# Fused window attention and Fourier gate: batch 0's queries and keys read in six-token rows, attention output of batches 2 and 3 turned by the DMA crossbar

## The chip, the cores and the metric

The kernel runs on one core of one Trainium2 chip. The metric is device time in microseconds (us) of one execution. Three runs of the kernel before gave 176.44, 176.39 and 172.52 us (median 176.39). The profile that all rows below come from is one more execution, of 173.44 us, whose traced span is 171.7 us.

## The reference, cut to what matters

There are 4 batches, 8 heads, 768 tokens and a head width of 64; q, k and v are float32. A query sees the first 8 keys of its sequence (global) and the 96 keys up to its own position (local), with a distance bias per head. The output feeds a second block of width 512.

```python
# attention, per batch and head
scores = q @ k.T / 8 - slope[h] * dist        # kept: key < 8, or 0 <= query - key < 96
a = softmax(scores);  x = a @ v               # x: [4, 768, 512] once heads are joined
# second block
x1, x2, x3 = split(x @ w_proj, 3)             # three projections of width 512
conv = irfft(rfft(x2, axis=1) * rfft(filter_fft, axis=1))    # over the 768 tokens
out = (x1 * conv * x3) @ w_out
```

## The kernel before, in words

**Attention.** The 768 tokens of a batch are cut into seven key tiles of 128 rows. Rows 0 to 7 of a tile repeat the 8 global keys, the other 120 are the tile's own; the last tile starts at token 648 and so overlaps the sixth. A key tile meets at most 216 queries. The tiles form three groups `c`: (0, 1), (2, 3), (4, 5, 6). Heads are handled in four pairs, 64 partitions to each head.

For batches 1 to 3, GpSimd (POOL) issues one DMA per tile of q, k or v, which also turns float32 into float16 (`load_rows`, `load_q`, line 322). Each row of a head is a piece of its own, of 256 bytes in DRAM: 960 pieces for a k or v tile, 1,024 for one of the six q tiles of 128 rows. The global rows are copied by DMAs that SyncE (SP) issues. There is one buffer each for `qn` and `kn`, so a batch's loads wait until the batch before has been transposed out of them; `vn` has two. For batch 0, SP loads q as float32 into the output staging tiles `ot`, and TensorE transposes it as float32 (`turned32`, line 639).

Scores need q and k with the head width on the partitions. `turned` (line 652) does that with TensorE transposes against an identity, and ScalarE (ACT) or VectorE (DVE) moves the result from PSUM into `QT` and `KT`. Batch 3 (`CROSS`) has it done by the DMA crossbar instead, with nine transposing DMAs on SP (`crossed`, lines 626 and 629). Then come score matmuls (line 693), the exponential on ACT (707, 12 to a batch), the mask product on DVE (724; in batch 0 the bias is added by matmuls instead, 684), the value matmuls (742 and 747, 65 columns, where the 65th is the sum of the weights), the reciprocal (771) and the scaling into `xn` (766 on DVE, or 770 on ACT).

`transpose_x` turns `xn` into `xT`, tokens along the free axis: TensorE transposes (787), and ACT or DVE copies 480 or 576 columns out of PSUM (306). That makes two groups of transposes and two copies per group `c`, 24 copies in all.

**Second block.** `gate` multiplies `xT` by the outer thirds of `w_proj` (856, four matmuls of 384 columns to a gate) and keeps x1·x3 in `g`. `butterfly` forms sums and differences of the three token thirds on DVE (801 to 812). `conv` projects them (925), goes to the spectrum (613), multiplies by the filter on DVE (1076 to 1096), comes back (950, 953), joins the halves (1033 to 1052), multiplies by `g` (1056) and projects out (977) into `ot`, which SP stores (985).

**Order.** Nothing is scheduled at build time or on the chip. The text `ORDER` lists every operation by number, with its engine (P, V, A, G, S) and, for matmuls, the PSUM banks it takes, and each engine executes its own sequence of it in order. An operation whose data are late holds up everything behind it on its engine. Batches overlap: while batch b is in its second block, batch b+1 is loaded, scored and weighted. Matmuls on zeros (`busy`, line 302) fill the wait at the start.

Of the kernel before, what the change touches and what calls it, by code (L numbers as in the profile page):

```python
# [39 lines left out]
0V 42V 3V 7V 27S 59S 28S 60S 61S 26S 69S 4G 54A 48A 45A 56A 50A 5V 1V 6V 29G 30G 66G 33G 65G 77G i6b1 17P0 18A  # L40
58A 47A 46A 43A 19V 11V 12P1 13A 49A 44A 57A 2A 14V 8V 15V 16A 55A 53A 20V 34V 39A 21A 51A 52A 22A 36A 37A 10V
40V 35G 70G 71G 72G 32G 68G 67G 73G i15b3 120P2 121V 9V 41V 93P3 94A 97P1 98V 82V 38V 258G 31G 74G 75G 267G
266G 226P0 95P4 96A 99A 230A 100P5 i1b6 122P2 123A 87A i1b1 126P3 127V 231V 269G i2b1 124P4 125V 101V 62V 64V
229V 268G 257G 255G 256G 259G 79G 76G 78G 80G 81G 262G i2b1 128P67 129A 134P23 135A 91P1 92V 24V 63V 132P45
133A 130P67 131A 102P23 103A 168P1 169V 227V 106P45 107A 170P6 171V 232V 166P7 167A 172P1 173V 228V 25V 261S
260S 263S 264S 275G 274G 273G 272G 265G 104P23 105A 108P45 109A 176P67 177A 178P01 179A 86A 136P23 137V 138V
141P45 142V 143V 174P67 175A 83A 115P23 116V 117V 110P01 111V 112V 180P45 181A 139P6 140A 89A 88A 144P7 145V
182P23 183V 184V 118P0 119A 85A 113P1 114V 187P45 188V 189V 383P7 185P6 186A 84A 384A 385P2 386V 213V 152P3
190P4 191V 212V 219V 215V 220V 357P6 147P2 149A 358A 154A 355P5 356V 198P4 200A 90A 359P2 360V 222V 214V 488G
271G 270G 496G 487G 489S 484G 495G 485G 193P7 195A 162P3 164A 396P01 397A 398V 216V 221V 364P45 361P67 362A  # L50
365A 208P2 210A 151P3 153V 366V 223V 23V 224V 225V 217V 146P0 148A 161P1 163A 165V 150V 218V 157P4 159A 370P67
393P23 394A 395V 367P01 368A 371A 192P5 194V 369V 372V 196V 156P4 158A 160V 155V 363V 233V 234V 235V 236V 237V
238V 239V 297P2 295P3 296A 387P01 388A 298A 390P67 280P4 281A 293P3 294A 391A 207P0 299P1 308P2 309A 300A
306P3 307A 301P5 203P4 205A 302A 284P2 285A 431P1 429P3 430A 432A 202P4 204V 209V 433P5 434A 490S 504G 486G
277G 503G 501G 276G 278G 506G 502G 494G 498G 378P67 379V 380V 392V 389V 252P23 253A 254A 240P4 241V 244P1 245A
246P5 247A 248P67 250A 249A 242P0 243A 373P23 374V 375V 206V 211V 719G 282P1 435P45 436A 283A 399P67 400V 401V
251V 441P23 442A 197P0 199A 404P45 405V 310V 406V 722G 491G 493S 720S 492S 381P1 382V 376P6 377A 288P7 289A
402P2 403V 443V 286P0 287A 583P3 407P4 408A 585P5 586V 437V 290V 584V 291V 303V 438P67 439A 440V 304V 292V
444P01 587P2 588A 445A 446V 311V 715G 717S 716G 409P4 419P5 410P6 412A 421A 420P7 595P23 596A 422A 598P01 599A
425P6 424P5 426A 427A 411A 447P23 448V 305V 449V 611P7 612A 723G 497G 279G 452P01 453V 454V 728G 505G 714G  # L60
500G 659P6 660A 324P5 314P4 315A 320P7 321V 428V 600V 312P2 316P3 317A 325A 313A 450P6 661P4 662A 318P0 455P3
456V 423V 201V 451V 478V 477V 413V 597V 479V 326P5 327A 319A 322P7 415P1 417A 323A 589P23 592P45 593A 811S
414P6 416A 468P0 470A 590A 458P1 460A 613P7 614V 418V 480V 328V 329V 481V 482V 594V 330V 483V 331V 591V 332V
457P6 459A 657P0 658A 729G 507G 734G 713G 712G 499G 730G 726G 727G 725G 732G 731G 724G 735G 733G 473P2 475A
618P45 619A 620V 333V 335V 621P67 615P01 616A 622A 463P3 472P2 474A 462P4 464A 465A 512P5 513A 521P6 522A
669P01 670A 624P23 625A 626V 525P7 526A 523P6 524A 672P45 663P01 664A 508P2 509A 673A 601P67 602V 334V 603V
623V 336V 665V 617V 671V 510P3 511A 467P0 536P1 537A 666P45 667A 668V 838S 718S 814S 813S 812S 837S 882S 721S
839S 883S 340P2 341A 469A 514P1 516P3 517A 515A 632P67 604P2 534P0 535A 538V 633V 674V 527P4 528A 605A 343P3
344A 606P01 607V 634V 608V 518V 352P5 353A 354S 529P4 530A 675P23 676V 519V 471V 635P5 636A 677A 627P67 609P4
610V 680P01 681V 628V 629V 532V 682V 531V 539V 520V 533V 346P5 337P4 338A 347A 339S 345S 342S 348S 349P6 630P7  # L70
631A 821P23 824P01 825A 350A 822A 351S 678P4 679V 826V 683P5 638P7 640A 684A 705V 653P0 548P6 546P1 547A 549A
550P2 544P3 554P7 555A 551A 545A 552P4 553V 706V 708V 707V 466V 461V 709V 476V 542P1 543A 655A 686P5 688A
691P4 693A 643P2 645A 540P3 541A 556V 843P67 840P01 841A 849P45 850A 647P2 649V 637P3 639A 844A 652P0 654V
823V 557V 558V 710V 559V 842V 560V 641V 711V 701P1 703A 893P45 846P23 847A 894A 815P67 736P0 737A 816A 817V
648P1 650A 749P2 890P45 891A 750A 696P3 698A 762P0 763A 832P67 833V 563V 651V 834V 561V 848V 892V 564V 753P1
754A 642P4 644A 751P5 752A 887P23 888A 884P01 818P67 819A 820V 845V 851V 895V 656V 740P4 741A 764P5 738P2 739A
885A 765A 766V 695P3 697A 700P4 742P2 743A 827P67 828V 829V 889V 886V 562V 757P0 758A 580P5 581A 702A 744P1
685P0 687A 755P5 756A 830P4 831A 745A 857P23 858V 859A 896P67 897V 898V 901P45 902V 903A 746V 747V 760V 689V
568P0 565P1 852P67 853V 854V 759V 748V 767V 571P2 572A 577P3 578A 860P4 690P5 861V 761V 835P2 836A 566A 855P3
856A 904P6 905A 899P7 900V 927V 926V 646V 929V 928V 930V 931V 704V 932V 574P2 575A 576S 567S 573S 582S 768P1  # L80
782P4 770P6 771A 569A 570S 579S 774P3 780P2 778P7 779A 783A 769A 868P6 776P0 777A 775A 772P7 773A 781A 784V
785V 786V 699V 787V 788V 791V 862P4 950P1 951A 933P7 934A 692A 694V 789V 792V 937P0 948P1 949A 938A 946P5
935P7 936A 947A 954P1 955A 867P0 952P3 959P5 961P7 962A 869A 953A 960A 872P1 874V 957V 956V 958V 963V 964V
941P2 942A 864A 870A 917P7 939P0 940A 943V 944V 945V 802P1 803A 805P5 878P6 863P4 865A 877P0 980P1 981V 866V
790V 971P4 972A 919A 879A 880A 808P3 984P4 978P2 982P7 983A 979A 967P1 968V 985V 986V 965P0 966A 969P6 970A
973V 881V 974V 975V 987V 976V 988V 977V 1004V 989V 799P7 793P4 794A 800A 801S 795S 804S 873P6 875A 809A 876V
871V 916P2 918A 796P1 797A 991V 990V 992V 993V 994V 920V 1006V 798S 810S 921P4 912P0 914A 911P3 913A 806A 923A
807S 922P2 906P1 908A 924A 925V 915V 907P3 909A 910V 1007V 1005V 1001P0 1002A 1003S 995P1 996A 997S 998P2 999A
1000S 1008P0 1009V 1010S 1014P1 1015V 1016S 1011P3 1012A 1013S
# [108 lines left out]
class Fused:  # L198
# [11 lines left out]
    CROSS = (3,)  # L210
    LATER = ()
# [8 lines left out]
    def __init__(self, ctx, tc, q, k, v, n_global, n_local, w_proj, filt, w_out, out):  # L220
# [10 lines left out]
        self.K0 = [KL * t for t in range(6)] + [S - KL]  # L231
# [6 lines left out]
    def buffers(self):  # L238
# [5 lines left out]
        self.qn = t("qn", [P, 6, H, D])  # L244
        self.kn = t("kn", [P, 7, H, D])
        self.vn = [t(f"vn{i}", [P, 7, H, self.VD]) for i in range(2)]
        self.QT = t("QT", [P, 4, S])
# [4 lines left out]
        self.xn = [t(f"xn{i}", [P, 2, 7, 2, D]) for i in range(2)]  # L252
# [12 lines left out]
        self.h1 = t("h1", [P, 6, DM])  # L265
        self.h2 = t("h2", [P, 6, DM])
# [24 lines left out]
        self.wide_dg = self.mix.bitcast(BF16).rearrange("p a b c -> p (a b c)")[:, 0:648]  # L291
        self.cst = t("cst", [1, 4])
        self.one = t("one", [1, P])
# [31 lines left out]
    def load_rows(self, what, dst, src, b, t):  # L325

        lo, hi = self.K0[t], self.K0[t] + KL
        self.load("G", dst[P - (hi - lo):P, t, :, 0:self.D],
                  src[b, :, lo:hi, :].rearrange("h p d -> p h d"), [what + (t,)], (8 * (hi - lo), 256),
                  f"load{what}{t}")  # L330

    def load_run(self, what, dst, src, t, n):

        rows = src[0, :, self.K0[t]:self.K0[t] + KL * n, :].rearrange("h (t p) d -> p t h d", t=n)
        self.load("G", dst[NG:P, t:t + n, :, 0:self.D], rows, [what + (i,) for i in range(t, t + n)],
                  (8 * KL * n, 256), f"load{what}{t}")

    def load_q(self, b, t):
        src = self.q[b, :, P * t:P * t + P, :].rearrange("h p d -> p h d")
        if b == 0:  # L340
            st = self.ot[t].rearrange("p (h d) -> p h d", h=self.H)
            self.load("S", st, src, [("ot", t)], (1024, 256), f"q{t}")
            if self.Q32:
                return
            self.g.op("AV", {"A": act(512), "V": 0.7}, lambda e: self.copy(
# [26 lines left out]
    def setup(self):  # L372
# [6 lines left out]
        def rows(_):  # L379
            row = self.row  # L380
            v.memset(row[:, 4, 0:1], 0.0)
            for n in (1, 2, 4, 8, 16, 32, 64):
                v.tensor_scalar(row[:, 4, n:2 * n], row[:, 4, 0:n], float(n), None, op0=Alu.add)
# [857 lines left out]
```

## Time and profile before

| what | value |
|---|---|
| profiled execution / its traced span | 173.44 us / 171.7 us |
| TensorE matmuls (PE), busy share of the span | 162.3 us, 95% |
| VectorE (DVE) | 156.7 us, 91% |
| ScalarE (ACT) | 151.1 us, 88% |
| GpSimd (POOL) | 77.4 us, 45% |
| first exponential / last of batch 0's value matmuls | 17.5 us / 29.8 us |
| first projection of batch 3 | 138.4 us |
| end of the last matmul / last copy out of PSUM starts | 167.8 us / 167.9 us |

A row of the groups reads: line, engine, operation, out<-in, partitions x elements and type, how often, then busy us and mean ns of one, and the idle time in front. A row of the chain reads: start, duration, engine, output and line. Instructions of one engine overlap a little at their ends, and matmuls a lot: one of 128 columns is recorded with 219 ns, while the chain has six of them in 0.34 us. So the cost of a matmul is read from the chain, and the sum of ACT or DVE durations is slightly more than the time they take. The PE's busy share counts a matmul until its result is out and is higher than the share in which it streams columns.

### The profile page before, as it was taken

The page shows a single profiled execution, that of the slowest core. Times are in us where ns is not written, and L with a number is a line of the kernel's source. Part 1 is how long each engine was busy: PE and PEld are TensorE (multiplying, and loading weights), DVE is VectorE, ACT ScalarE, POOL GpSimd, SP SyncE. Part 2 cuts the span into 40 slices and gives each one's busy share as a digit, 9 for nine tenths or more (in the row PEclk, how much of TensorE's full clock was granted, in tenths as well). Part 3 has the DMA queues.
Part 4 walks back from the last instruction along what each step waited for, and adds up shares of the span by engine and source line. Part 5 has one row for each costly group of instructions (what it writes and reads, how often), then busy time and mean ns, then how long its engine had stood idle before and what let it go on. Part 6 is the DMA issues. An engine that isn't in the chain of part 4 may idle for free.

```text
span 171.7 us, 4390 instructions
## 1 busy us (share of the span) xinstructions
PE 162.3 (95%) x1675; PEld 102.2 (60%) x1675; DVE 156.7 (91%) x355; ACT 151.1 (88%) x309; POOL 77.4 (45%) x95
## 2 busy tenths in 40 slices
PE   6888899999999979999999999999999999999990
PEld 1365689865464757965455767654576745575540
DVE  7997989989999899999999998999989999999960
ACT  5799999999899979999999999999998986866841
POOL 8999999962499994948993000000000000000000
PEclk9999999999999999999999999999999999999999
DMA  6999999999999999999999996500000360000854
GB/s 127 181 207 151 144 154 146 169 203 187 148 151 142 144 144 135 87 140 137 156 151 134 153 188 199 230 4 0 0 4 0 117 256 0 0 0 28 308 217 186
DMA packets 98077, 22.44 MB, mean 131 GB/s; under 512 B 90808, under 2 KB 94984, under 8 KB 98056
## 3 DMA queue, kind: packets, MB, share of 16 engines
q0 software_dynamic: 80912, 12.14, 100.3%
q1 hardware_dynamic: 17144, 10.02, 22.2%
q8 instruction: 13, 0.21, 0.5%
q14 instruction: 8, 0.07, 0.1%
HBM read 25.84 MB, written 6.29 MB: 187 GB/s over the span
## 4 chain that ended last, share of the span: by engine, by line
PE 72%; DMA 6%; POOL 6%; DVE 6%; ACT 6%; issue 2%; ACTq 0%; DVEq 0%
PE bank L856 23%; PE bank L925 9%; PE bank L977 9%; PE bank L950 5%; PE bank L693 5%; PE bank L613 5%; PE bank L652 4%; DMA QT<-qn 3%; PE bank L787 3%; PE bank L742 3%; DMA qn<-in_q_dram 3%; POOL kn L322 3%; PE bank L747 3%; POOL vn L322 2%; PE bank L684 2%
## 5 line engine op out<-in xcount | busy, mean ns | idle before, releaser
L856 PE MATMUL bank<-xT,w 128*128 128x384 f16 x256 | 47.4, 326 | 0.0
L707 ACT ACTIVATE E<-bank 128x864 f16<-128x864 f32 x48 | 41.4, 917 | 0.7 <-ACT h L310 0.3
L856 PEld LDWEIGHTS <-w 128*128 128x128 f16 x256 | 23.8, 98 | 16.3 <-issue 1.1
L322 POOL DMA_DIRECT2D vn<-in_v_dram x28 | 25.7, 923 | 4.4 <-DMA g<-in_moe_filter_fft_dram 3.9
L322 POOL DMA_DIRECT2D kn<-in_k_dram x28 | 25.9, 934 | 2.7 <-PE bank L856 2.2
L977 PE MATMUL bank<-wo,y 128*128 128x512 f16 x96 | 22.8, 379 | 0.0
L724 DVE TENSOR_TENSOR E<-E,mask 128x864 f16<-128x864 f16 x36 | 20.8, 603 | 0.8 <-ACT E L707 0.8
L322 POOL DMA_DIRECT2D qn<-in_q_dram x18 | 16.3, 917 | 6.1 <-PE bank L652 5.6
L310 ACT ACTIVATE ot<-bank 128x512 f32<-128x512 f32 x22 | 13.3, 618 | 4.6 <-PE bank L977 4.0
L866 ACT CAST g<-bank 128x384 f16<-128x384 f32 x32 | 15.9, 536 | 1.1 <-PE bank L856 0.9
L310 ACT ACTIVATE ab<-bank 128x512 f16<-128x512 f32 x24 | 14.2, 619 | 2.6 <-PE bank L925 2.5
L766 DVE TENSOR_TENSOR xn<-bank,rc 128x512 f16<-128x512 f32 (+1 forms) x21 | 16.0, 764 | 0.5
L742 PE MATMUL bank<-vn,E 128*128 128x65 f16 x224 | 15.3, 193 | 0.0
L742 PEld LDWEIGHTS <-E 128*128 128x128 f16 x224 | 14.0, 97 | 1.9
L747 PE MATMUL bank<-vn,E 128*128 128x65 f16 x192 | 15.1, 193 | 0.0
L977 PEld LDWEIGHTS <-y 128*128 128x128 f16 x96 | 8.9, 98 | 9.3 <-DVE y L1056 0.2
L693 PE MATMUL bank<-QT,KT 64*128 64x216 f16 (+2 forms) x224 | 13.9, 241 | 0.3 <-DMA QT<-qn 0.3
L306 ACT CAST X<-bank 128x512 f16<-128x512 f32 x24 | 13.6, 610 | 0.6 <-PE bank L613 0.5
L310 ACT ACTIVATE x<-bank 128x384 f16<-128x384 f32 x25 | 12.5, 526 | 1.3 <-DVE g L868 1.0
L747 PEld LDWEIGHTS <-E 128*128 128x128 f16 x192 | 13.2, 97 | 0.5
L306 ACT CAST eo<-bank 128x384 f16<-128x384 f32 x27 | 11.5, 508 | 1.4 <-PE bank L953 1.4
L693 PEld LDWEIGHTS <-KT 64*128 64x128 f16 x224 | 8.5, 94 | 6.3 <-issue 4.4
(142 smaller groups left out, 354.8 us busy)
## 6 DMA issues: line engine op xcount, KB each, us to landing
out_dram<-ot SPq DMA_DIRECT2D x24, 256.0 KB
kn<-in_k_dram POOLq DMA_DIRECT2D x28, 120.0 KB, 5.4
vn<-in_v_dram POOLq DMA_DIRECT2D x28, 120.0 KB, 5.2
qn<-in_q_dram POOLq DMA_DIRECT2D x18, 128.0 KB, 5.3
ot<-in_q_dram SPq DMA_DIRECT2D x6, 256.0 KB
w<-in_moe_w_proj_dram POOLq DMA_DIRECT2D x4, 256.0 KB, 6.7
g<-in_moe_filter_fft_dram POOLq DMA_DIRECT2D x1, 768.0 KB, 14.1
w<-in_moe_w_proj_dram POOLq DMA_DIRECT2D x1, 512.0 KB, 9.4
```

The lines of the kernel that those rows point to most:

```text
L306: {"A": nc.scalar.copy, "V": nc.vector.tensor_copy, "G": nc.gpsimd.tensor_copy}[e](out, in_)
L310: self.nc.scalar.mul(out, in_, c)
L322: return self.g.op(eng, 0.57 + 0.00035 * nbytes[0] if eng == "G" else 0.5, lambda _: e.dma_start(dst, src), w=w, r=r, nbytes=nbytes, name= ...
L693: nc.tensor.matmul(bs[hh].f32()[:, off:off + w], self.KT[hs, m, hp], self.QT[hs, hp, KL * m:KL * m + w], start=(off == 0 and not near), st ...
L707: g.op("A", act(864), lambda _: nc.scalar.activation(eo, bs[0].two()[:, :, 0:432].rearrange("p h (m w) -> p h m w", m=2), Act.Exp, scale=s ...
L724: g.op("V", dve(864, 2), lambda _: nc.vector.tensor_mul(eo, eo, mk), r=[("mask", 2 * hp), ("mask", 2 * hp + 1)], w=[("E", hp, gi)], name=" ...
L742: nc.tensor.matmul(o[:, n, hh], ef[:, at:at + P], vt[:, t, 2 * hp + hh, 0:D + 1], start=first, stop=(t == 0), skip_group_check=True)
L747: nc.tensor.matmul(o[:, n, hh], ef[:, at:at + P], vt[:, t - 1, 2 * hp + hh, 0:D + 1], start=False, stop=True, skip_group_check=True)
L766: nc.vector.tensor_mul(to, o[:, :, :, 0:D], rc.to_broadcast([P, 2, 2 * nt, D]))
L856: nc.tensor.matmul(bk.f32()[:, 0:h], self.w[:, c, o + P * j:o + P * j + P], self.xT[:, c, h * s:h * s + h], start=(c == 0), stop=(c == 3))
L866: g.op("A", act(h), lambda _: nc.scalar.copy(x3, pts[1].f32()[:, 0:h]), use=[pts[1]], w=[ko], name="x3")
L977: nc.tensor.matmul(bk.f32(), y[:, c, P * t:P * t + P], self.wo[:, c, :], start=(c == 0), stop=(c == 3))
```

## The change

1. **Batch 0's q and k** arrive in eight DMAs on POOL, one for each head pair of q and of k. Partition p gets tokens 6p to 6p+5 of two heads, so a piece is 1,536 bytes of DRAM instead of 256 (`load_six`). `six` transposes each pair with 12 TensorE transposes, 64 data columns each, and two copies put the columns back in token order in `QT` or `KT`, with steps of six elements. SP's six q loads, the float32 transposes and the seven k loads of 120 rows go.
2. **Tiles of 48 rows.** The last k and v tile holds only tokens 720 to 767. q is tiled like k, seven tiles of 120 and 48 rows, and `QT` has the layout of `KT`. A score matmul that ran over 216 or 168 queries is now two, of 120 and of 96 or 48.
3. **Crossbar for `xn`.** In batches 2 and 3 (`XX`) TensorE's transposes and the copies out of PSUM go. `xn` is one tile, laid out for it, and SP issues one transposing DMA per token tile, seven to a batch (`crossed_x`). The scaling into `xn` on DVE takes two instructions in place of one. The next batch's scaling waits until the crossing of the same group has read `xn`.
4. Batch 3's nine crossings of q and k are four (`QX`, `KX`).
5. **Setup.** The index rows are made by 9 instead of 16 small DVE instructions; the slope tables by 8 products of 128 rows on ACT and DVE instead of 16 of 64 rows on ACT; one activation table load goes; the memsets on `vn` and `kn` shrink.
6. The last output tile is made in two halves of 256 columns. The filter spectrum is kept in smaller tiles.
7. `ORDER` is new throughout: the filter and batch 0's spectrum work stand earlier, 14 instead of 27 matmuls on zeros are left, and much of the rest has moved.

```diff
+    XX = (2, 3)
-        self.K0 = [KL * t for t in range(6)] + [S - KL]
+        self.K0 = [KL * t for t in range(6)] + [S - 48]
...
+    def load_six(self, what, dst, src, i):
+        self.load("G", dst[:, i], src[0, 2 * i:2 * i + 2].rearrange("h (p r) d -> p h r d", r=6),
+                  [(what + "six", i)], (256, 1536), f"six{what}{i}")
...
-    def turned32(self, t):
+    def six(self, what, i):
...
+            for r in range(6):
+                for hh in range(2):
+                    nc.tensor.transpose(b.f16()[64 * hh:64 * hh + 64, P * r:P * r + P], buf[:, r, hh], self.ident)
...
+        def move(e):
+            self.copy(e, dst[:, 0:6, i, lo:lo + KL].rearrange("p m (c r) -> p r m c", r=6),
+                      view(0, 120).rearrange("p r (m c) -> p r m c", m=6))
+            self.copy(e, dst[:, 6, i, end[0]:end[1]].rearrange("p (c r) -> p r c", r=6), view(120, P))
...
-                for hh in range(2):
-                    hs = slice(64 * hh, 64 * hh + 64)
-                    nc.tensor.matmul(bs[hh].f32()[:, off:off + w], self.KT[hs, m, hp],
-                                     self.QT[hs, hp, KL * m:KL * m + w], ...)
+                for x in range(1 + (w > KL)):
+                    n = w - KL if x else min(w, KL)
+                    for hh in range(2):
+                        hs = slice(64 * hh, 64 * hh + 64)
+                        nc.tensor.matmul(bs[hh].f32()[:, off + KL * x:off + KL * x + n], self.KT[hs, m, hp],
+                                         self.QT[hs, m + x, hp, 0:n], ...)
...
+    def crossed_x(self, c):
+        for t in self.GRP[c]:
+            at, n = KL * t - 8 * (t % 2), (P if t % 2 else P - 16) if t < 6 else 48
+            self.g.op("S", 1.25, lambda _, at=at, n=n, t=t: self.nc.sync.dma_start(
+                self.xT[:, :, at:at + n], self.xn[0:n, t].rearrange("p h d -> p (h d)"), transpose=True),
+                nbytes=(4 * n, 256), name="crossx", r=[("xn", j, c) for j in range(2)],
+                w=[("xT", j, c, t) for j in range(2)])
...
             for j in range(2):
                 self.values(j, c, b % 2)
-                self.transpose_x(j, c)
+                if b not in self.XX:
+                    self.transpose_x(j, c)
+            if b in self.XX:
+                self.crossed_x(c)
...
+            for lo, hi in ((0, 256), (256, 512)) if last and t == 5 and self.HALVES else ((0, 512),):
```

## The prediction

> **What bounds the kernel now.** I read the page's engine shares first, then the busy time by stretches, then the chain that ended last, and the groups by shape for prices.
>
> ```profile
> PE 162.3 (95%) x1675; PEld 102.2 (60%) x1675; DVE 156.7 (91%) x355; ACT 151.1 (88%) x309; POOL 77.4 (45%) x95
> ```
>
> Three engines are nearly full, so no single one can be named from the page. The stretches (length; then busy us of PE, weight loads, DVE, ACT, POOL; granted clock; DMA share; GB/s) part them:
>
> ```profile
> 40.00:50.00 10.00, 10.00 (x74) 5.36 (x74) 9.83 (x22) 9.52 (x18) 5.70 (x7) 1.00 2.10 159
> 120.00:130.00 10.00, 10.00 (x133) 6.50 (x132) 9.33 (x20) 9.60 (x30) 0.00 (x0) 1.00 0.01 2
> 150.00:160.00 10.00, 10.00 (x74) 6.37 (x72) 9.71 (x25) 6.10 (x15) 0.00 (x0) 1.00 0.16 61
> ```
>
> In the middle DVE and ACT, which empty PSUM, are busy 93 to 98%; what is taken off both shortens it. The PE's full marks there are recorded latencies: 133 matmuls in the second row, most of them of 65 columns, cannot fill 10 us at the 30 ns at which such matmuls follow each other. After 138 us ACT has slack, and the chain is PE without a break:
>
> ```profile
> 77.42 0.24 PE bank L652 x4
> ...
> 86.16 2.66 POOL kn L322 x3
> 88.82 5.37 DMA qn<-in_q_dram
> 94.19 5.77 DMA QT<-qn
> 100.09 0.55 PE bank L693 x8
> ...
> 138.36 5.18 PE bank L925 x24
> ...
> 158.71 3.90 PE bank L856 x24
> 162.62 5.19 PE bank L977 x24
> 167.88 0.60 ACT ot L310
> ```
>
> This also gives true prices: 216 ns for 512 columns (L977, L925), 163 ns for 384 (L856), 55 to 60 ns for a 128-column transpose (L652). The 77 to 100 us pieces say that batch 3's first scores wait for its loads, one after another on POOL, and then for the crossbar.
>
> **The change part by part.**
>
> *Front, to the first exponential.* ACT is the engine that is late here: from 5.2 us on it hardly stops until the first exponential.
>
> ```profile
> 1.76 1.28 ACT L310 ACT_TABLE_LOAD   x1 [1.76 <-DVE eo L381]
> 17.50 4.78 ACT L707 ACTIVATE E<-bank 128x864 f16<-128x864 f32 x6
> ```
>
> By the new order, ahead of that point ACT loses one table load (1.28 us), 12 of 16 slope products (3.4 us for 16, so 2.6), two spreads of the distance table (0.7), one table copy (0.5), three q casts (590 ns each less overlap, 1.5), one k copy (0.3) and one mask (0.7): 7.6. It gains four pairs of six-step copies, 720 and 48 columns. No row shows a stepped copy on either engine; the nearest, 576 columns at 696 ns and 1,024 at 1,017 ns, give 0.8 for 720, and 64x64 at 248 ns gives 0.2 for 48. That is 3.0 with overlap taken off to 4.0 without, and four more table and first-row copies at 0.4 each, 1.6. Net -2.0 to -3.0. The first angle matmul, which waited for the index rows until 4.78 us, also comes sooner. Against it stand the loads: POOL issues eight pair loads of 256 pieces. A load of 960 pieces costs it 0.93 us, one of 512 pieces (w) 0.82, so 256 cost some 0.75; with 4.2 us of distance tables in between, the last pair is issued at about 11.6 us, and at 5.4 us to landing arrives at 17. Three pairs are there by 12, enough to start. Values of batch 0 are then issued from 15 to 23 us instead of 13.6 to 20.7, with the filter ahead of them. I take -2.0; the bounds are 0 (the loads decide) and -3.6.
>
> *Transposes of batch 0.* 24 float32 and 28 float16 transposes go (24 x 0.11 + 28 x 0.056 = 4.2 us), 96 with half the output partitions come. The nearest row is line 460, four of this shape in 0.30 us with 0.22 us latency: 28 to 56 ns each, 2.7 to 5.4. Zero net on a PE that waits for ACT here.
>
> *Scores.* 192 more matmuls, the same columns. Pairs for two heads run side by side (eight of 216 columns in 0.48 us with latency). If every short one cost the 29 ns of a 65-column matmul, the sum would be 5.6 us of PE; if columns count, 0. They stand where PE waits for exponentials, and are hidden by those; without that cover 5.6 is their price. I take 0.
>
> *Crossbar for xn.* The copies that go, half of these rows:
>
> ```profile
> L306 ACT COPY xT<-bank 128x480 f16<-128x480 f16 x10 | 5.9, 585 | 2.1 <-PE bank L787 2.1
> L306 ACT COPY xT<-bank 128x576 f16<-128x576 f16 x3 | 2.1, 696 | 0.0
> L306 DVE COPY xT<-bank 128x480 f16<-128x480 f16 x6 | 2.3, 400 | 0.0
> L306 DVE COPY xT<-bank 128x576 f16<-128x576 f16 x5 | 2.3, 454 | 0.2 <-ACT eo L306 0.2
> L766 DVE TENSOR_TENSOR xn<-bank,rc 128x512 f16<-128x512 f32 x15 | 10.2, 687 | 0.3
> L766 DVE TENSOR_TENSOR xn<-bank,rc 128x768 f16<-128x768 f32 x6 | 5.7, 957 | 0.1
> ```
>
> Six on ACT (5 x 0.585 + 0.696 = 3.6) and six on DVE (3 x 0.400 + 3 x 0.454 = 2.6): 6.2 us. The scaling on DVE in two parts pays its fixed cost twice: from the two L766 rows, 0.15 us plus 1.05 ns an element, over eight groups that is 1.2 us, less 0.7 for one group that goes to ACT, where four more small products cost 0.9. Seven q tiles instead of six make copies of batches 1 and 2 longer, 0.7. Net 6.2 - 0.5 - 0.9 - 0.7 = 4.1 over two engines that share their work, so -2.0. The 56 PE transposes (3.1 us) lie behind these engines and count nothing. What comes is SP's time:
>
> ```profile
> L629 SPq DMA_TRANSPOSE QT<-qn x6: 1192/1515/2042, 88.9 to 103.5; - x6
> ```
>
> Seven per batch take 8 to 14 us of SP, and the last of a group lands some 1 us after its issue ends. A group of three is thus ready 5 to 7 us after `xn`, where transposes and copies took 1.5 to 2. In the new order, counted with these rows, 11 us of other DVE work stand between the last reciprocal of batch 3 and its butterfly (before, 4.7), so I count the latency at nothing; uncovered it costs 3 to 5 us a batch. Behind a crossing on SP stand later crossings and output stores; six staging tiles hide the stores. The added wait, scaling of batch 3 until batch 2's crossing has read `xn`, would hold all of DVE; batch 2's crossings are a whole batch older.
>
> The Trainium skill, "VectorE: DVE Perf Modes", section "The three transpose paths", speaks against this step: it lists 390 ns for a 128x128 transpose on TensorE, 1309 ns by DMA, and advises TensorE where PSUM will do. By that figure 28 blocks a batch would take an estimated 37 us, which no cover could hide; the row above has four blocks in 1.2 to 2.0.
>
> *Tail.* From 138.36 us the chain holds 29.5 us of PE: all the projections, spectrum and output of batch 3, 24 output matmuls of batch 2, and 56 gate matmuls left over. The new order has 40 gate matmuls after that point: 16 x 0.163 = 2.6 less. They run earlier, where PE has gaps; half of it may only move, so -1.3 (0 to -2.6). The half-size last copy (0.60 against about 0.4) gives -0.2.
>
> *Loads.* POOL issues as long as before: 60 of 120 rows, 10 of 48 (about 0.78), 8 pairs, 68.4 us against 74 x 0.92 = 68.1. Nothing, up to -1 where buffers come free sooner.
>
> **The sum.** -2.0 - 2.0 - 1.3 - 0.2 = -5.5. Against the profiled execution, 173.44 us, that is **168.0 us**. That execution lies 1.7% under the median of the runs shown, 176.39; two of three lie there, so a median may come out up to 3 us higher for the same work. Two per cent is about what a measurement here can tell from nothing.
>
> **Rivals.**
>
> *The loads take the front back (no change).* For: POOL waits 5.6 us for qn's transposes in the trace, and batch 3 starts on loads; batch 0's values are now issued 2 us later, the gates' weights after them. Against: scores start on three pairs. Without the front's -2.0 and the tail's -1.3 the time is 171.3. The shorter front decides nothing if the first gate stays at its present 31 us.
>
> *The crossings come late (slower).* Batch 2's last three crossings stand on SP behind batch 3's crossings of 16 and 20 blocks, which wait for loads that end now at 94 to 99 us. If those end no sooner, they follow at about 102.5, take 3 x 2.04 + 1 = 7.1, and the butterfly, at 103.8 now, starts at 109.6: +5.8. With the same 3 to 5 us uncovered in batch 3, the time is 168.0 + 5.8 + 5 = 178.8. It is slower than before once the two delays exceed 5.5 us in sum, and over 2% slower from 9.
>
> *The change does less than it says.* Stepped copies at twice the price (8 x 0.8 = 6.4 us over two engines, +3.2) and the short score matmuls at half their bound (+2.8) would give 174.0: no change.
>
> **How the numbers follow.** The forecast's case, 164 to 170, has 0.62. No change, from the first and third rival, has 0.24; late crossings 0.14. All gains at their bounds are 3.6 + 4.1 + 2.6 + 0.2 + 1 = 11.5, or 162. The range runs from 163 to 176: it takes in the no-change cases and the higher median, and leaves out most of late crossings and the very end of the gains.
>
> **What would show it.** Right: first exponential near 15.5 us; first projection of batch 3 near 134; a last stretch of 27 us of PE; fewer than 0.5 us of DVE idle before the butterflies of batches 2 and 3. Wrong: DVE or PE idle released by DMA xT<-xn, PE idle before batch 0's values or first gates released by loads, stepped copies over 1 us. The prediction fails if SP's queue, not DVE and ACT, sets the middle.

## The result and the profile after

The change makes the kernel slower: 181.89 us median (180.54 to 182.6) against 174.45 of the kernel before on the same chip, a ratio of 1.054 with a 95% interval of 1.042 to 1.066. Some executions of one and the same kernel are 1 to 3% slower than its others, and every ratio here is taken from the faster ones of both kernels, so it can differ from the quotient of the two medians beside it. The forecast was 168.0, with 176 as the upper end. The profiled execution took 181.34 us, its span 179.5.

The first two lines of the page of the changed kernel (busy time of each engine; granted TensorE clock in 40 slices):

```profile
PE 163.1 (91%) x1854; PEld 104.0 (58%) x1854; DVE 157.8 (88%) x361; ACT 154.6 (86%) x299; POOL 75.3 (42%) x99
...
PEclk9995555999999999999999999999999999999999
```

The shares are lower only because the span is longer: DVE and ACT, from which work was to be taken, are each busy for more us than before (156.7 and 151.1). The clock is at half in four slices of the front. Its stretches, in the columns shown for the kernel before:

```profile
10.00:20.00 10.00, 3.40 (x66) 2.71 (x60) 3.33 (x17) 9.96 (x14) 8.69 (x11) 0.69 1.32 154
20.00:30.00 10.00, 8.08 (x117) 6.66 (x114) 9.88 (x13) 8.44 (x11) 7.59 (x10) 0.50 2.11 157
...
120.00:130.00 10.00, 10.00 (x110) 5.46 (x105) 9.66 (x18) 9.61 (x17) 0.00 (x0) 1.00 0.28 107
```

From 10 to 20 us ACT is full, DVE is busy a third of the time and TensorE a third; in the kernel before, the same stretch had 8.07 us of TensorE and 8.37 of DVE beside 9.89 of ACT. From 20 to 30 us DVE is full with 13 instructions. That is nearly 0.8 us each. From 120 to 130 us both are as full as they were. The groups by shape over the first 40 us name what fills them in the front:

```profile
L314 ACT COPY KT<-bank 128x720 f16<-128x720 f16 x2 | 5.2, 2582 | 0.5 <-PE bank L651 0.5
L314 ACT COPY QT<-bank 128x720 f16<-128x720 f16 x2 | 5.1, 2544 | 0.0
L314 DVE COPY KT<-bank 128x720 f16<-128x720 f16 x2 | 5.2, 2606 | 0.0
L314 DVE COPY QT<-bank 128x720 f16<-128x720 f16 x2 | 5.1, 2560 | 0.0
...
L314 ACT COPY KT<-bank 128x48 f16<-128x48 f16 x2 | 1.1, 552 | 0.0
```

A stepped copy (one that writes every sixth place) of 720 columns takes 2.54 to 2.61 us where the prediction put 0.8, on both engines alike, and one of 48 takes 0.45 to 0.55 in place of 0.2. The timeline of ACT (start, length) has the first exponential at 24.4 us, 17.5 before:

```profile
23.10 1.28 ACT L727 ACT_TABLE_LOAD   x1
24.40 1.89 ACT L727 ACTIVATE E<-bank 128x864 f16<-128x864 f32 x2
```

The chain that ended last carries the copies one after another, then two pieces of the middle, then the tail:

```profile
12.69 2.62 ACT KT L314 x2
...
16.71 2.61 ACT QT L314 x2
...
20.33 2.69 DVE KT L314 x4
23.02 2.63 DVE QT L314 x2
26.30 2.73 DVE QT L314 x2
29.05 2.61 DVE KT L314 x3
...
92.04 11.67 DMA QT<-qn
...
148.61 5.18 PE bank L965 x24
...
170.92 4.33 PE bank L1020 x20
...
175.81 0.71 ACT ot L318 x2
```

Read along the two kernels (start of the same work, before and after): first exponential 17.5 and 24.4; last reciprocal of batch 0 at 30.3 and 41.4; batch 1's first projection copy at 82.2 and 88.0; batch 3's first exponential 100.7 and 104.25; batch 3's first projection 138.4 and 148.6; span 171.7 and 179.5. The front loses 11 us, and the tail gains 2.3 (29.5 us from that projection to the last copy, now 27.2). The marks between do not say where the rest is won or lost, because the new order puts other work between them: from batch 3's first exponential to its first projection there are 88 gate and 44 output matmuls where there were 72 and 24, which is 6.9 us of TensorE at 0.163 and 0.216 us each, and that stretch is 6.7 us longer.

The copies that went are gone as forecast. These groups answer to the `xT` and `xn` rows of before:

```profile
L314 ACT COPY xT<-bank 128x480 f16<-128x480 f16 x5 | 2.9, 571 | 0.3 <-PE bank L816 0.3
L314 ACT COPY xT<-bank 128x576 f16<-128x576 f16 x2 | 1.3, 660 | 0.0
L795 DVE TENSOR_TENSOR xn<-bank,rc 128x256 f16<-128x256 f32 x10 | 3.7, 413 | 0.1
L795 DVE TENSOR_TENSOR xn<-bank,rc 128x384 f16<-128x384 f32 x6 | 2.9, 540 | 0.0
```

### The profile page after: what moved, and what is told of

The parts are those of the page before. It is cut to its first block, busy times and chain, and to the rows that moved or that the text cites. A ratio compares the mean times of both kernels' runs of the same rounds, so it can differ in the third digit from the quotient of the medians.

```text
span 179.5 us, 4745 instructions
## 1 busy us (share of the span) xinstructions
PE 163.1 (91%) x1854; PEld 104.0 (58%) x1854; DVE 157.8 (88%) x361; ACT 154.6 (86%) x299; POOL 75.3 (42%) x99
## 4 chain that ended last, share of the span: by engine, by line
PE 72%; DVE 12%; DMA 7%; ACT 6%; issue 2%; ACTq 0%
PE bank L893 21%; PE bank L1020 11%; PE bank L965 9%; DMA QT<-qn 7%; PE bank L990 5%; PE bank L616 4%; PE bank L714 4%; PE bank L678 4%; PE bank L310 3%; DVE QT L314 3%; PE bank L764 3%; DVE KT L314 3%; PE bank L769 3%; ACT KT L314 2%; PE bank L816 2%
## 5 line engine op out<-in xcount | busy, mean ns | idle before, releaser
L330 POOL DMA_DIRECT2D kn<-in_k_dram x25 | 21.5, 863 | 10.8 <-PE bank L678 9.0
L330 POOL DMA_DIRECT2D qn<-in_q_dram x25 | 21.4, 859 | 7.7 <-PE bank L616 4.3
L1020 PE MATMUL bank<-wo,y 128*128 128x512 f16 (+1 forms) x100 | 22.9, 371 | 0.0
L318 ACT ACTIVATE ot<-bank 128x512 f32<-128x512 f32 (+1 forms) x24 | 13.7, 593 | 4.8 <-PE bank L1020 4.2
L714 PEld LDWEIGHTS <-KT 64*128 64x128 f16 x416 | 12.5, 100 | 8.6 <-issue 7.4
L714 PE MATMUL bank<-QT,KT 64*128 64x120 f16 (+2 forms) x416 | 16.1, 214 | 1.5 <-DMA QT<-qn 1.3
L314 ACT CAST eo<-bank 128x384 f16<-128x384 f32 x30 | 13.4, 519 | 2.9 <-issue 1.6
L318 ACT ACTIVATE x<-bank 128x384 f16<-128x384 f32 x28 | 14.0, 533 | 0.3 <-PE bank L893 0.2
L314 ACT CAST X<-bank 128x512 f16<-128x512 f32 x21 | 11.6, 629 | 0.2 <-PE bank L616 0.2
L990 PE MATMUL bank<-inv,X 128*128 128x256 f16 x64 | 11.2, 272 | 0.0
```

The costliest lines, as they stand in the source:

```text
L314: {"A": nc.scalar.copy, "V": nc.vector.tensor_copy, "G": nc.gpsimd.tensor_copy}[e](out, in_)
L318: self.nc.scalar.mul(out, in_, c)
L330: return self.g.op(eng, 0.57 + 0.00035 * nbytes[0] if eng == "G" else 0.5, lambda _: e.dma_start(dst, src), w=w, r=r, nbytes=nbytes, name= ...
L714: nc.tensor.matmul(bs[hh].f32()[:, off + KL * x:off + KL * x + n], self.KT[hs, m, hp], self.QT[hs, m + x, hp, 0:n], start=(off == 0 and x ...
L990: nc.tensor.matmul(o[:, 0:P] if z else o[:, P:3 * P], X[:, s, cs], self.inr[:, s - 4] if z else self.inv[:, (s + 2) % 4], start=(n == 0), ...
L1020: nc.tensor.matmul(bk.f32()[:, 0:hi - lo], y[:, c, P * t:P * t + P], self.wo[:, c, lo:hi], start=(c == 0), stop=(c == 3))
```

## The experiments

Two theories stood first. A: the price of the stepped copies is the loss. B: the late crossings and the new order are, and the front's delay would be swallowed anyway.

### What the stepped copies cost

**Plain copies.** In `six`, the copies run through both sides in order, which leaves batch 0's tokens mixed up:

```diff
-            self.copy(e, dst[:, 0:6, i, lo:lo + KL].rearrange("p m (c r) -> p r m c", r=6),
-                      view(0, 120).rearrange("p r (m c) -> p r m c", m=6))
+            self.copy(e, dst[:, 0:6, i, lo:lo + KL], b.f16()[:, 0:720].rearrange("p (m c) -> p m c", m=6))
...
```

> The changed kernel, with the eight pairs of copies of batch 0 reading and writing runs of 120 and 48 columns in place of steps of six. It leaves out the putting back of batch 0's queries and keys into token order, so that their attention is taken between mixed-up tokens; loads, matmuls, order and sizes stay. Theory A (the stepped copies are what the change loses): the copies fall from 2.57 us to 0.7 to 0.8 and from 0.5 to about 0.35, the first exponential comes at 16 to 18 us instead of 24.4, batch 0's attention ends 8 to 11 us sooner, and the time falls from 181.9 to 170 to 174. Rival B (the late crossings and the new order lose it, and the front's delay would be swallowed later anyway, as half of it is by batch 2): the time stays at 177 or more.

Measured: 172.87 us against 172.89, a ratio of 0.991 (0.985 to 0.996). The first exponential came at 16.4, and the copies took 0.75 us on ACT and 0.53 on DVE:

```profile
L314 ACT COPY QT<-bank 128x720 f16<-128x720 f16 x2 | 1.5, 748 | 0.0
L314 DVE COPY QT<-bank 128x720 f16<-128x720 f16 x2 | 1.1, 528 | 0.0
```

Theory A stands, with 9 us by the medians and 11 by the ratios; B falls as the main cause.

**The loops exchanged.** The write is dense now (to neighbouring places), and the read of PSUM jumps 256 bytes from element to element; all is computed:

```diff
-            self.copy(e, dst[:, 0:6, i, lo:lo + KL].rearrange("p m (c r) -> p r m c", r=6),
-                      view(0, 120).rearrange("p r (m c) -> p r m c", m=6))
+            self.copy(e, dst[:, 0:6, i, lo:lo + KL].rearrange("p m (c r) -> p m c r", r=6),
+                      view(0, 120).rearrange("p r (m c) -> p m c r", m=6))
...
```

> The changed kernel, computing all, with the two loops of the stepped copies exchanged: the write goes through neighbouring 2-byte places, the read of PSUM jumps by 256 bytes from element to element. If the step of the write to SBUF sets the price (2-byte pieces 12 bytes apart), the copies fall to 0.8 us or near it. If any access that does not run through neighbouring places costs this much, whichever side it is on, they stay at about 2.5 us, and the time at 180 to 183. If PSUM is worse than SBUF at it, they cost over 3 us.

> The changed kernel with the copies' loops exchanged, computing all, for a time with an interval. One run gave 172.9 beside 172.9 before. The prediction's sum without its misprice would be 168 to 169, a ratio of 0.97; if the crossings eat the middle, it stays within 1% of before, 0.985 to 1.0.

Measured: 172.9 in the single run; then, repeated, 172.07 against 174.02, a ratio of 0.983 (0.978 to 0.989). Its groups by shape:

```profile
L314 DVE COPY QT<-bank 128x720 f16<-128x720 f16 x2 | 1.8, 902 | 0.0
L314 DVE COPY KT<-bank 128x720 f16<-128x720 f16 x2 | 1.8, 900 | 0.0
L314 ACT COPY KT<-bank 128x720 f16<-128x720 f16 x2 | 1.5, 759 | 0.5 <-PE bank L651 0.5
L314 ACT COPY QT<-bank 128x720 f16<-128x720 f16 x2 | 1.5, 748 | 0.0
```

The same elements, moved to the same places: 0.75 and 0.90 us in place of 2.55. The step of the read costs ACT nothing (0.75 with plain copies too) and DVE 0.37 us; the step of the write is what costs. This version is 6 to 7% faster than the change and 1 to 2% faster than the kernel before (0.983 here, 0.990 in a later run).

**A price by step.** The changed kernel with dense reads and other steps of the write:

```diff
...
+            n = {"q0": 2, "k0": 4, "q2": 8, "k2": 12, "q1": 2, "k1": 4, "q3": 8, "k3": 12}[what + str(i)]
+            self.copy(e, dst[:, 0:6, i, lo:lo + KL].rearrange("p m (c r) -> p r m c", r=n),
+                      b.f16()[:, 0:720].rearrange("p (r m c) -> p r m c", m=6, r=n))
```

> The changed kernel with the eight 720-column copies reading PSUM densely and writing 2-byte places at steps of 2, 4, 8 and 12 elements (4, 8, 16 and 24 bytes), one of each on ACT and on DVE; it leaves out the right token order of batch 0. If every jump of the write costs the same, all eight take about 2.55 us. If the price follows the number of new 16-byte lines that are entered (the Trainium skill, page "SBUF — State Buffer", says that leaving a line pays, without a price), steps of 4 bytes cost about a quarter of the extra 1.8 us, 1.2 us, steps of 8 bytes 1.6 to 1.7, and 16 and 24 bytes the most and alike, about 2.5 to 3.2.

Groups by shape, each in the stretch of one copy, so that steps are not mixed; in this order, on ACT steps of 24, 8, 4 and 16 bytes, and on DVE of 8, 4, 16 and 24:

```profile
L314 ACT COPY KT<-bank 128x720 f16<-128x720 f16 x1 | 3.3, 3329 | 0.5 <-PE bank L651 0.5
L314 ACT COPY KT<-bank 128x720 f16<-128x720 f16 x1 | 1.8, 1786 | 0.0
L314 ACT COPY QT<-bank 128x720 f16<-128x720 f16 x1 | 0.9, 948 | 0.0
L314 ACT COPY QT<-bank 128x720 f16<-128x720 f16 x1 | 3.3, 3340 | 0.0
L314 DVE COPY KT<-bank 128x720 f16<-128x720 f16 x1 | 1.7, 1748 | 0.0
L314 DVE COPY QT<-bank 128x720 f16<-128x720 f16 x1 | 0.9, 949 | 0.0
L314 DVE COPY QT<-bank 128x720 f16<-128x720 f16 x1 | 3.4, 3371 | 0.0
L314 DVE COPY KT<-bank 128x720 f16<-128x720 f16 x1 | 3.4, 3418 | 0.0
```

The price grows with the step up to 16 bytes and stays there at 24. It fits a price for each 16-byte line entered: 720 writes at 4 bytes enter 180 of them, at 16 bytes 720, so (3.34 - 0.95) / 540 = 4.43 ns a line, and 0.15 us remain. From these two, 8 bytes (360 lines) come to 1.75 and 12 bytes (540 lines) to 2.54: measured 1.75 to 1.79, and 2.54 to 2.61 in the changed kernel. The 48-column copies do not lie on this line: 36 lines would make 0.31 us, and they took 0.45 to 0.55. The expectation by lines was right in form; its figures were 0.25 us high at 4 bytes and at least 0.15 low at 16. The Trainium skill, "SBUF — State Buffer", section "Specifications (TRN2)", has the rule: 16-byte lines, at least two hits on each for full speed, a penalty for each crossing. It gives no price; these rows do, and they do not show its threshold: at 8 bytes each line gets two hits and the copy takes 1.75 to 1.79 us, at 4 bytes it gets four and the copy takes 0.95.

**The step on TensorE's side.** Products with the identity write float32 PSUM at every sixth place of two banks, and the copies read it densely:

```diff
-                    nc.tensor.transpose(b.f16()[64 * hh:64 * hh + 64, P * r:P * r + P], buf[:, r, hh], self.ident)
+                    for bk, lo, n in ((b, 0, 60), (b2, 60, 68)):
+                        nc.tensor.matmul(bk.f32()[64 * hh:64 * hh + 64, r:6 * n:6], buf[:, r, hh],
+                                         self.ident[:, lo:lo + n], start=True, stop=True, skip_group_check=True)
```

> The changed kernel, computing all, with the step moved from the copies to TensorE: products with the identity write float32 PSUM at every sixth place over two banks (60 and 68 columns each, 24 matmuls for 12 transposes), and the copies read dense runs of 360. Theory A: copies of 0.75 to 0.85 us, the time as with plain copies, 170 to 174, unless TensorE writes stepped columns slowly; 192 matmuls of 64 columns at 30 ns are 0.72 us for each group of 24, and over 2 us a group would mean that the step costs there too. Rival B: 177 or more.

Measured: 175.74 against 172.89, 1.014 (1.008 to 1.021). 24 matmuls took 0.86 us, 12 whole transposes 0.53, so no price of the stepped write into PSUM shows beside the number of matmuls; 24 dense ones were not run. The copies took 0.75 and 0.90. Better than the change, but above A's range of 170 to 174 (and under B's 177): by the ratios 2% behind the plain copies and 3% behind the exchanged loops, with copies as long as theirs. Why was not settled.

**The half clock.** 33 idle matmuls more, in TensorE's waits between 10 and 25 us:

```diff
-... 207P0 ... 89P3 ... 84P1 ... 94P3 ...
+... i7b6 207P0 ... i7b6 89P3 ... i14b6 84P1 ... i5b6 94P3 ...
```

> The changed kernel with its stepped copies as they are, and 33 more idle matmuls of 512 columns in the waits of TensorE between 10 and 25 us, where its granted clock is 0.5. If the copies themselves set the front, nothing moves, 180.5 to 182.5, though the clock shows 1.0. If the half clock is a good part of the loss (scores of batch 0 at 0.9 us a pair in place of 0.55, the exponentials waiting for them), 177 to 179.5.

Measured: 179.98 against 173.72, 1.040 (1.034 to 1.046), between the two expectations. The stretches of this run:

```profile
10.00:20.00 10.00, 9.02 (x94) 4.76 (x90) 3.95 (x17) 9.96 (x14) 8.64 (x11) 1.00 1.31 157
20.00:30.00 10.00, 5.72 (x123) 4.32 (x120) 9.90 (x13) 9.26 (x11) 7.34 (x9) 1.00 2.10 159
```

The clock is at 1.00 and the copies are as full as ever: the first exponential came at 24.4 again, batch 0's last reciprocal at 41.1 (41.4 without). So the half clock went with TensorE's waiting (3.40 us busy from 10 to 20 us, 9.02 here) and cost the front 0.3 us at most. This ratio is 1.4% under the change's, but the two intervals overlap, and no more is read from it.

### What the crossbar is worth

**Without it.** The changed kernel, with turns and copies of batches 2 and 3 back on TensorE, DVE and ACT; each turn is put two matmul groups behind its scaling, or behind the last gate that still reads the old `xT`:

```diff
-    XX = (2, 3)
+    XX = ()
```

> The changed kernel with its front as it is, but xn of batches 2 and 3 turned by TensorE and copied by ACT and DVE again, as in batches 0 and 1, in an order in which each turn stands two matmul groups behind its scaling. Theory A: the front's loss stays and the crossbar's gain goes, 182 to 185. Rival B (late crossings lose it): b2's butterfly comes 8 us or more sooner than at 120 us, and the time falls under 177.

> The same without the crossbar for xn in either batch. Prediction's term: 2 us more than with it, 174.5 to 176. Rival (the crossbar costs as much as it gives): 171 to 173. With the copies' loops as the change has them, leaving the crossbar out gave 191.3 against 181.9; if that order of turns is what costs and not the copies, this run comes out 8 to 10 us above 172.9 too, and the gap opens behind xT copies.

> The changed kernel with the copies' loops exchanged, and xn of batch 2 turned by TensorE again; only batch 3 uses the crossbar, when no loads are under way. Prediction's term: DVE and ACT get 3 us of copies back, 1.5 us slower, 174 to 175. Rival (crossings of batch 2 run beside batch 3's loads and hold them up): the first crossing of batch 3's queries lands in 6 to 8 us in place of 12.9, the gap of PE and ACT at 90 to 105 us closes, and the time is 169 to 172.

Measured: 191.28 against 172.89 with the stepped copies (1.108, 1.103 to 1.114). With the loops exchanged, 181.75 against 173.72 without any crossing (1.049, 1.042 to 1.056) and 179.71 with batch 3 alone crossed (1.039, 1.032 to 1.045); with both it was 0.983. All three are slower than either theory's figure. They are no clean price, since turns that have to wait for late gates of the batch before stand in TensorE's queue in an order made for crossings. But one reading is clean: in the run with batch 3 alone, no crossing of `xn` stands beside the first crossing of batch 3's queries, and this still landed after 12.43 us (11.91 in the run with stepped copies and no crossing of `xn` at all, 11.7 to 12.9 with both batches crossed). So the crossings of `xn` are not what makes that one late. What the crossbar is worth in the changed kernel stays open.

**The crossbar part alone.** The kernel before, with the new layout of `xn`, the shifted values and `crossed_x` for batches 2 and 3, each transfer put on SP's queue as soon as its scalings are done, and nothing else moved:

```diff
+    XX = (2, 3)
...
-                self.transpose_x(j, c)
+                if b not in self.XX:
+                    self.transpose_x(j, c)
+            if b in self.XX:
+                self.crossed_x(c)
```

> The kernel before, with one part of the change alone: xn of batches 2 and 3 laid out by tokens and turned by the crossbar, each group's transfers issued on SP's queue as soon as both scalings are done, nothing else moved; the 24 turns and copies go. The prediction's term: 6.2 us of copies less 2.1 of dearer scaling over two engines, 2 us faster, so 170.5 to 171.5 against 172.9. Rival (crossings and loads share the DMA engines: in the last kernels the first crossing of batch 3's queries took 12.9 us to land, 5.8 in the kernel before): batch 3's first scores wait 4 to 7 us longer, the butterflies of batches 2 and 3 wait for xT by 2 us or more each, and the time is 176 to 182.

Measured: 191.39 against 173.72, 1.110 (1.100 to 1.120), far above even the rival's 176 to 182. The waits name it, in us in total, times, longest:

```profile
DVE xab L816 <- DMA xT<-xn: 13.2, 1, 13.2
...
DVE xab L818 <- DMA xT<-xn: 5.2, 1, 5.2
```

and the chain shows what batch 2's crossings stood behind:

```profile
100.04 1.32 SPq L627
101.48 1.20 SPq L627
102.77 1.21 SPq L804
104.03 1.26 SPq L804
105.38 0.53 SPq L1004
106.02 1.22 SPq L804
107.28 2.37 DMA xT<-xn
```

L627 is batch 3's query crossings and L804 the crossings of `xn`. Queued behind the former, batch 2's butterfly waits 13.2 us and batch 3's, whose seven crossings go out one by one, 5.2: 18.4 us in sum, about as much as the whole difference of 17.7. This is the prediction's late-crossings rival, which was priced at 5.8 and 5, in an order that has no cover. The changed kernel's order has that cover. All that DVE waits for `xT` in it is

```profile
DVE xab L838 <- DMA xT<-xn: 0.3, 1, 0.3
```

so the rival is not what made it slow.

### What the middle loses

With the loops exchanged the kernel gains 2 to 3 us of the 5.5 forecast. The chain has, in that kernel:

```profile
22.44 6.54 DMA vn<-in_v_dram
...
82.53 12.32 DMA QT<-qn
```

The second piece is the first crossing of batch 3's queries, 12 blocks of 128 x 128 in one transfer. It is counted from its issue on; TensorE itself waits 1.6 us for it.

**One exchange on SP's queue.** Batch 2's last three crossings before the 20-block crossing of keys, in the written order (`793S 660S 661S 662S 791S` for `793S 791S 660S 661S 662S`).

> The same with one exchange on SP's queue: batch 2's last three crossings of xn before the 20-block crossing of batch 3's keys, which now stands between them and their scalings. If the place behind the large crossing holds up batch 2's butterfly (112.0 us now, 8.7 us after the scaling), the butterfly comes 2.5 to 3.5 us sooner and the time falls by 1 to 2.5 us. If batch 3's second group of scores then waits as much, nothing moves, within 0.5.

Measured: 175.55 against 174.02, 1.005 (1.000 to 1.010), 2% worse than without. The butterfly came 1.1 us sooner (110.6), and the keys then arrived late: the chain shows 4.86 us of DMA KT<-kn, TensorE idle 2.7 us from 110 to 115. The second theory had the wait, but not that it costs more than it gives; the large crossing was in the right place.

**Size or traffic.** Three runs. The first leaves out most of batch 3's value loads (one row in place of 120):

```diff
+        if what == ("vn", 1) and b == 3:
+            r0 = P - 1
```

The second splits the crossing:

```diff
-    QX = ((0, 3), (3, 7))
+    QX = ((0, 1), (1, 2), (2, 3), (3, 7))
```

The third leaves the crossing whole and leaves out most of what is loaded beside it:

```diff
+        if b == 3 and (t > 1 or what[0] == "vn") and t < 6:
+            r0 = P - 1
...
-        n = KL if t < 6 else 48
+        n = (1 if b == 3 and t > 2 else KL) if t < 6 else 48
```

It was run again on one chip with the whole kernel as its control.

> The same, leaving out nearly all of batch 3's value loads: 8 pieces for each tile in place of 960, so that batch 3 attends to values of batch 1. If loads beside the crossing are what makes the first crossing of batch 3's queries land after 12.9 us (5.8 before), it lands in 5 to 8, the idle 90 to 95 us goes, and the time falls to 168 to 170.5. If the crossing of 12 blocks takes that long by itself, it stays at 11 or more, and the time at 172 to 173.

> The changed kernel with the copies' loops exchanged, and the first crossing of batch 3's queries, 12 blocks in one transfer, in three transfers of four blocks, one after the other in the same place on SP's queue. If the size of the transfer makes it land after 12.3 us, the first scores of batch 3 start 3 to 5 us sooner (near 91 us in place of 94.9), the idle of PE and ACT at 90 to 95 us goes, and the ratio falls from 0.983 to 0.965 to 0.975. If it is the traffic beside it, three small ones last as long, 0.98 to 0.99.

> The same with the 12-block crossing whole, leaving out nearly all of batch 3's loads that are issued from 75 us on: its values, and its queries and keys from the third tile on, 8 pieces for each tile in place of 960, so that batch 3 works mostly on batch 2's rows. If traffic makes the crossing late, it lands in 4 to 6 us in place of 12.3, and the ratio is 0.96 to 0.97. If 12 blocks take that long by themselves, it still takes 10 to 12 us, and the ratio stays above 0.973.

> The changed kernel with the copies' loops exchanged, computing all, as the control beside the next run on one chip. 0.980 to 0.990 of the time before.

> The same without batch 3's loads from 75 us on (its values, and queries and keys from the third tile on, 8 pieces for each tile in place of 960). On another chip it had the same ratio as the control, 0.983, though its span was 2.4 us shorter and its idle at 90 to 100 us was gone. If the loads' traffic is what the middle loses, it is 1 to 2% under the control here; if not, within 0.5%.

Measured: without the values 0.977 (0.971 to 0.983), and the crossing still took 11.34 us, as the second theory has it; the time is not clear of the 0.983 (0.978 to 0.989) with them. Split 0.998 (0.994 to 1.001), worse, so neither theory's figure came. Three transfers held SP for 8.54 us in place of 3.6 to 3.7; TensorE is still idle for 2.3 us from 90 to 95, and the chain names another transfer there, a copy of value rows that SP issued just before them (10.62 us of DMA vn<-vn). Nothing waits for the queries in that run, so it does not say whether size plays a part. Quiet 0.983 (0.978 to 0.989) on another chip; side by side on one chip, 171.96 for the control (0.990, 0.985 to 0.995) and 169.66 for the quiet one (0.978, 0.972 to 0.983). The two stretches, with all loads:

```profile
90.00:95.00 5.00, 3.45 (x50) 2.07 (x47) 4.69 (x13) 3.08 (x7) 0.00 (x0) 1.00 1.85 144
95.00:100.00 5.00, 5.00 (x52) 2.61 (x53) 3.93 (x8) 4.58 (x8) 0.00 (x0) 1.00 1.89 149
```

and without batch 3's late ones:

```profile
90.00:95.00 5.00, 5.00 (x63) 2.69 (x61) 5.00 (x10) 4.96 (x9) 0.00 (x0) 1.00 0.49 62
95.00:100.00 5.00, 5.00 (x81) 4.05 (x80) 4.60 (x13) 4.26 (x9) 0.00 (x0) 1.00 0.91 170
```

The crossing is off the chain, the DMA share falls from 1.85 to 0.49, and ACT's idle of 1.9 us goes. Batch 3's late loads are worth 2.3 us here. That takes in every wait for them; the crossing's own part is not shown, since nothing waits for it in the quiet run.

### What the front loses

**Without batch 0's values**, alone and together with the quiet middle:

```diff
+        if what == ("vn", 0) and b == 0 and t < 6:
+            r0 = P - 1
```

> The changed kernel with the copies' loops exchanged, leaving out nearly all of batch 0's value loads (8 pieces for each tile in place of 960; VectorE clears the six tiles instead, 1 to 2 us of its time in its idle 11 to 15 us). With all loads the chain of waits shows 6.5 us of a value load at 22.4 us, and batch 0's last reciprocal starts at 30 to 34 us, 30.3 before, although the first exponential came 0.4 to 1.9 us sooner. If the loads take the front's gain back (the prediction's first rival), batch 0's last reciprocal comes at 27.5 to 29, and the ratio falls from 0.983 to 0.990 to 0.965 to 0.978. If the front's gain is lost in front of the scores, nothing moves.

> The same, and batch 3's loads from 75 us on left out as well (its values, queries and keys from the third tile on). If both stretches of waiting for loads are what separates the priced-right kernel from the prediction's 168.0 against a profiled 173.4 (0.969), their gains add: 0.955 to 0.968.

Measured: 171.84 against 173.15, 0.996 (0.992 to 1.000), and 168.76, 0.978 (0.974 to 0.982). Batch 0's last reciprocal came at 30.1 and 30.2 us; with all loads it came at 30.0, 31.5 and 34.1 in three profiles. Neither gain came: without the values the time is that of the kernel with all loads (172.07 and 171.96), although the ratio is higher, and nothing adds to the quiet middle. The second run is 3.1 us faster than the first, which leaves out the same loads but for batch 3's: the quiet middle's gain, seen a second time. In the first of these runs the chain names the filter's load (10.73 us) and one of the gates' weights (8.05) in their place.

## Why the prediction was wrong

**The step that failed** is the price of the stepped copies in "Front, to the first exponential": "No row shows a stepped copy on either engine; the nearest, 576 columns at 696 ns and 1,024 at 1,017 ns, give 0.8 for 720, and 64x64 at 248 ns gives 0.2 for 48." They measured 2.54 to 2.61 and 0.45 to 0.55. On ACT four pairs cost 4 x (2.56 + 0.54) = 12.4 us where "3.0 with overlap taken off to 4.0 without" stood. With that, the prediction's own sum for the front is 12.4 + 1.6 - 7.6, 6.4 us later than before; measured 6.9, which is 8.9 behind the forecast 15.5. DVE's four then stood in a row from 20.3 to 31.6 us. With the write made dense and nothing else changed, the ratio fell from 1.054 to 0.983. The bound itself was the fault: the price of an unseen form was put down with no upper end but the nearest rows, and the third rival tried twice that, where three times came true.

**What bounds the kernel.** Right for the front, and what made the error dear: ACT was late there, so every us of the copies on ACT went on the path. For the middle, "what is taken off both shortens it" is not confirmed. With dense writes DVE and ACT have 5.0 and 4.1 us less to do than before (151.7 and 147.0), yet batch 3's first projection starts at 139.9 in that profile, 138.4 before, with 12 gate matmuls (2.0 us) more ahead of it. Of the -4.0 forecast for front and crossbar some -0.5 is left at that point, and the gain over the kernel before is the tail's.

**Transposes and short scores.** Counted at nothing; no run parts them. The 12 transposes of a pair take 0.53 us with latency.

**The crossbar's work.** Right in size: copies of xT went from 8.0 to 4.2 us on ACT and from 4.6 to 1.9 on DVE, 6.5 together (forecast 6.2); the scalings cost 1.0 more on ACT (0.9) and 0.2 less on DVE (0.5 more).

**"I count the latency at nothing."** Wrong in its place. The butterflies were covered, as reckoned (DVE waits 0.3 us for `xT` in the changed kernel, 0.4 in the profile with dense writes). The uncovered wait is that of batch 3's first scores for the 12-block crossing of its queries, 1.6 us of TensorE with dense writes, which the prediction did not price. The late loads as a whole are worth 2.3 and 3.1 us in two pairs of runs.

**Tail.** 29.5 us from the first projection to 27.2: -2.3, forecast -1.3 with bounds 0 and -2.6. In the trace 44 gate matmuls are left there, not the 40 of the prediction, so 12 x 0.163 = 2.0 of it are theirs, and they moved ahead of that point. The half-size last copy gave nothing: from the last matmul to the end of the span it is 4.3 us where it was 3.9.

**Loads.** By the prices named for it the sum is 69.0 us of POOL, not 68.4; nothing rests on it.

**The sum without the mispriced term** would have been too good all the same: measured 0.983 and 0.990, that is 2 to 3 us, of 5.5. Without batch 3's late loads it is 4.3. In the front the first exponential comes 0.4 to 1.6 us sooner than before, and batch 0 ends no sooner; what takes that back is open (batch 0's values alone do not), and so is where the rest is lost.

**The rivals.** "The change does less than it says" named the right term with too small a price. "The crossings come late" was a real mechanism, shown at 18.4 us in the kernel before, but the changed order covers it. "The loads take the front back" was not confirmed for the values, and not tried for the filter and the weights.

**The signs** worked: "stepped copies over 1 us" and a first exponential far from 15.5 pointed at the cause at once, and "a last stretch of 27 us of PE" came out, though the time did not.

## What to carry to other kernels

Price an access pattern that no row shows by the 16-byte lines that its write enters, and put the loop whose step is smallest in the output innermost; a stepped read of PSUM cost nothing on ACT and 0.37 us on DVE, where a stepped write into SBUF cost three to five times the dense copy. Look for such a form first on the engine that is late. When work is moved onto a queue, price each wait for what else stands on that queue and for the traffic beside it, not for the transfer alone, and make the order anew.

## What the runs showed of the hardware

- A 16-bit copy of 720 columns that writes SBUF at steps costs 4.43 ns for each 16-byte line entered, beside 0.15 us, on ACT and DVE alike (0.95 us at 4 bytes, 1.75 to 1.79 at 8, 2.54 to 2.61 at 12, 3.33 to 3.42 at 16 and 24).
- A read of PSUM that jumps 256 bytes from one 16-bit element to the next cost ACT nothing (0.75 us) and DVE 0.37 us (0.90 in place of 0.53).
- TensorE wrote float32 PSUM at steps of 24 bytes at no visible price: 24 matmuls of 60 and 68 columns in 0.86 us.
- A crossing of 12 blocks landed after 11.7 to 12.9 us beside loads (11.3 without the value loads); where one of 20 blocks stood behind three others, the chain held 4.9 us of it.
